# A two-layer MoE behind attention: the second layer's tokens in two blocks (1024, 512) in place of three of 512

## Chip, cores and metric

One core of a Trainium2 chip runs the whole kernel in one launch. The metric is the device time of one execution in microseconds (us). TensorE (PE) multiplies, VectorE (DVE), ScalarE (ACT) and GpSimd (POOL) work element by element, SyncE (SP) issues the DMAs.

## The reference, cut to what matters

```python
def reference(...):
    x = _attn_ref(q, k, v, centroids)      # 2 x 8 heads, 768 tokens, 64 wide, masked by cluster
    x = x.transpose(0, 2, 1, 3).reshape(1536, 512)
    x = _moe_ref(x, w_in, w_out)           # layer one: elu(x @ w_in) @ w_out, 512 -> 2048 -> 512
    return _moe2_ref(x, domain_probs, w1, w2)

def _moe2_ref(x, domain_probs, w1, w2):    # layer two: 4 experts, each 512 -> 1024 -> 512
    p = domain_probs / (domain_probs.sum(-1, keepdims=True) + 1e-09)
    for e in range(4):
        h = np.maximum(x @ w1[e], 0.0)
        out += p[:, e:e + 1] * (h @ w2[e])
```

## The kernel before

All matrix products take fp32 operands split in a high part and a rest (both fp32r); a product is three matmuls: high by high, high by rest, rest by high. The kernel has three stages: attention (to about 390 us), layer one (`moe`, to about 540) and layer two (to the end). The order of instructions on each engine is the order in which the code emits them.

Both layers are a list `steps`. Layer one has 48 steps, numbered 0 to 47: 16 chunks of 128 features, in groups of 2, 4, 5 and 5 chunks, each group for the three token blocks of 512 in turn; the last five steps of block 0, 1 and 2 end at step 37, 42 and 47. A step is a first product (`emit_G1`, two steps ahead) and a second one (`emit_G2`). When a block has its last step, `acc[tb]` (512 tokens, channels in four tiles of 128) is layer two's input.

Layer two has 16 chunks of 256 features (four per expert), and in the version before 3 steps to a chunk, one for each block of 512 tokens. Its first product is a Strassen form (Winograd's): features, channels and tokens are halved, and seven products take the place of eight. `x2_make` makes a block's seven inputs A11, A12, A22, S1 to S4 (high part on ACT, rest on POOL or DVE, called low here), `w2_split` a chunk's weights. I call one of the seven products a pass: two halves of 128 channels by three matmuls, six matmuls into a PSUM bank. `quad_early` does passes one to five (into the banks px, pz, px, py, px), `quad_late` the sixth (px) and seventh (pz). ACT copies px out between passes (m1, u2, u3), DVE adds up the quarters (c11, c2, c1). A quarter's relu goes to ACT (h), the rest of it to DVE (l). So h0 is the first 128 features, h1 the second; a stands for the first half of the tokens, b for the second. The two products of neighbouring steps are laced: passes one to five of the next step, tile 0 of this step's second product, passes six and seven, tiles 1 to 3. A tile is 128 tokens: six matmuls of 512 columns, and then an eviction on DVE, which adds the PSUM bank, times `prob`, to `acc`. Five PSUM banks (`ps_a`) rotate over the tiles.

While layer one ends, `tick` walks through generators (`going`) piece by piece: a block's inputs, and the next chunk's weights. Before, blocks 0 and 1 have theirs made while layer one still runs, and block 2 during layer two's first steps.

Of the kernel before, what the change touches and what calls it, by code (L numbers as in the profile page):

```python
# [46 lines left out]
def kernel(  # L47
# [30 lines left out]
    ident = const.tile([128, 128], F32, name="ident")  # L78
    identb = const.tile([128, 128], BF16, name="identb")
    ramp = const.tile([128, 1, 2 * C], F32, name="ramp")  # L80
    cc = const.tile([128, HP, 4 * C], F32R, name="cc")
# [22 lines left out]
    def attention():  # L104
# [27 lines left out]

        kscale = fix.tile([4 * C, 1], F32, name="kscale")
# [485 lines left out]
    W2_TAGS = (early[:6], last[1:7])  # L619
    X2_TAGS = (  # L620
        ["qh", "ql", "kl"] + [f"x0{kk}" for kk in range(KD)],
        [f"x1{kk}" for kk in range(KD)] + early[6:] + last[:1],
        [f"x2{kk}" for kk in range(KD)] + last[7:],
    )
    A11, A12, A22, S1, S2, S3, S4 = range(7)
# [48 lines left out]
    def w2_split(n):  # L674
# [14 lines left out]
        for x, names in (  # L689
            (a[:, :, 0], ("B11", "B21")), (t[:, 0:2].rearrange("p a k f -> p (a k) f"), ("T1", "T2")),  # L690
            (t[:, 2:4].rearrange("p a k f -> p (a k) f"), ("T3", "T4")), (b22, ("B22",)),
        ):
            m = 2 * len(names)
            o = home(tags[len(ops) // 2], [128, 2, m, 128], "w1op")
# [4 lines left out]
        h, l = (home(tag, [128, 2, 512], "w2op") for tag in tags[4:])  # L699
# [46 lines left out]
    def moe():  # L746
# [8 lines left out]
        g_t, x2, x2_gen, w_gen2 = {}, {}, {}, {}  # L755

        def emit_G1(s):
# [12 lines left out]
            gh = gp.tile([128, 512], F32R, tag="gh", name="gh")  # L770
            gl = gp.tile([128, 512], F32R, tag="gl", name="gl")
            r = tp.tile([128, 512], F32, tag="r", name="r")
            gg = tp.tile([128, 512], F32, tag="gg", name="gg")
# [8 lines left out]
        def product(ps, a, b, s, start, stop):  # L782
            tb, n = steps[s][1:3]
            x, w = x2[tb][a], w_t[n][0][b]
# [7 lines left out]
        def quad_early(s):  # L792
            px, py, pz = (ps_h.tile([128, 256], F32, tag=f"h{i}", name="h") for i in range(3))
            u = [tp.tile([128, 2, 256], F32, tag=t, name=t) for t in ("r", "gg")]
            c = tp.tile([128, 512], F32, tag="r", name="c")
            m1, u2, u3, c11 = u[0][:, 0], u[0][:, 1], u[1][:, 0], u[1][:, 1]
# [9 lines left out]
            dve.tensor_tensor(out=c[:, 256:512], in0=pz, in1=u3, op=ALU.add)  # L806
            more(s, 2)
            return px, pz, u2, c11, c

        def more(s, n):  # L810

            if s == NS1 + 1:
                for _ in range(n):
                    next(x2_gen[NB - 1], None)

        def quad_late(s, px, pz, u2, c11, c):
            a, b = slice(0, 256), slice(256, 512)
            (h0, l0), (h1, l1) = g_t[s] = [
                (gp.tile([128, 512], F32R, tag="gh", name="gh"), gp.tile([128, 512], F32R, tag="gl", name="gl"))
                for _ in range(2)  # L820
            ]
            act.activation(out=h0[:, a], in_=c11, func=AF.Relu)
            product(px, A22, "T4", s, False, True)
            product(pz, S4, "B22", s, False, True)
            act.activation(out=h0[:, b], in_=px, func=AF.Relu)
# [6 lines left out]
            low(l0[:, a], h0[:, a], c11)  # L832
            low(l0[:, b], h0[:, b], px)
            more(s, 2)
            dve.tensor_tensor(out=c[:, a], in0=pz, in1=u2, op=ALU.add)
            act.activation(out=h1, in_=c, func=AF.Relu)
            low(l1, h1, c)
            more(s, 2)

        def x2_make(tb, t):  # L840
# [3 lines left out]
            x2[tb] = {}  # L844
            ends = tb == NB - 1
            if ends:

                o = moe_p["st"].tile([128, 2, 512, 2], I32, tag="st", name="st").bitcast(F32)
                o = o.rearrange("p i f t -> p (i f t)").rearrange("p (n k f) -> p n k f", n=4, k=2)
                sums = [o[:, n] for n in range(4)]  # L850

            def high(i, x):
                o = home(X2_TAGS[tb][i], [128, 2, 2, 256], "x2")
                x2[tb][i] = o[:, 0], o[:, 1]
                act.activation(out=o[:, 0], in_=x, func=AF.Copy)

            def low(i, x):
                h, l = x2[tb][i]
                if ends or i not in (S1, S2, S4):
                    pool.tensor_tensor(l, x, h.bitcast(F32), ALU.subtract)  # L860
                else:
                    dve.tensor_tensor(out=l, in0=x, in1=h.bitcast(F32), op=ALU.subtract)

            def both(i, x):
                high(i, x)
                low(i, x)

            def sum_of(x, y, op):
                o = sums.pop() if ends else tp.tile([128, 2, 256], F32, tag="xs", name="xs")
                dve.tensor_tensor(out=o, in0=x, in1=y, op=op)  # L870
                return o

            s1 = sum_of(a21, a22, ALU.add)
            if ends:

                s2 = sum_of(a11, s1, ALU.subtract)
                yield
                high(A11, a11)
                high(S1, s1)
                yield  # L880
                low(A11, a11)
                low(S1, s1)
                s4 = sum_of(a12, s2, ALU.add)
                yield
                high(S2, s2)
                high(A12, a12)
                yield
                low(S2, s2)
                s3 = sum_of(a11, a21, ALU.subtract)
                low(A12, a12)  # L890
                yield
                high(S3, s3)
                high(A22, a22)
                high(S4, s4)
                yield
                low(S3, s3)
                low(A22, a22)
                low(S4, s4)
                return
            both(A11, a11)  # L900
            yield
            s2 = sum_of(a11, s1, ALU.subtract)
            both(S1, s1)
            yield
            both(S2, s2)
            yield
            s4 = sum_of(a12, s2, ALU.add)
            both(A12, a12)
            yield
            s3 = sum_of(a11, a21, ALU.subtract)  # L910
            both(S4, s4)
            yield
            both(A22, a22)
            yield
            both(S3, s3)
# [3 lines left out]
        def emit_G2(s, ms=range(4)):  # L919
            ly, tb, n, opens, closes, first, final = steps[s]  # L920
            if opens and 0 in ms:
# [88 lines left out]
        for t in sorted(load_at):  # L1010
            if t < -2 * LAG:
                for n in load_at[t]:
                    w_load(n)
# [63 lines left out]
```

## Time and profile before

| | |
|---|---|
| median of 3 runs | 1048.33 us (1048.17 to 1050.28) |
| profiled execution, span from first to last instruction | 1049.3 us; its own time is not listed apart from the three runs |
| TensorE busy | 1030.4 us of it |
| VectorE, ScalarE, GpSimd busy | 737.4, 525.2, 397.5 us |
| matmuls | 6265 |

The span leaves out what lies ahead of the first and behind the last instruction on the chip; here it is 1.0 us above the median of the runs, and within their spread. A busy TensorE is not a TensorE at its peak: a matmul of 256 columns that waits for its weights counts as busy.

### The profile page before, as it was taken

Reading aid. Unit: us, or ns where it says so; the run is one execution under the profiler, and the core shown is the slowest. Engines: PE = TensorE matmul, PEld = TensorE weight load, DVE = VectorE, ACT = ScalarE, POOL = GpSimd, SP = SyncE. Lnnn points to the kernel's source line nnn. Section 1 sums busy time; section 2 is a strip of 40 time slices with the busy share of each in tenths; the row PEclk is TensorE's granted clock in tenths of the full one; section 3 lists DMA queues with packets and bytes.
Section 4 is the critical chain, followed back from the end, with each engine's and each line's share of the span. In section 5 each row is a group of like instructions: output and inputs, shape, how many; then the busy total and the mean of one; then the engine's idle time right before and its main releaser. Section 6 shows DMA issues by size and latency. Waiting matters only on the chain.

```text
span 1049.3 us, 16463 instructions
## 1 busy us (share of the span) xinstructions
PE 1030.4 (98%) x6265; PEld 919.9 (88%) x6265; DVE 737.4 (70%) x1243; ACT 525.2 (50%) x1081; POOL 397.5 (38%) x398
## 2 busy tenths in 40 slices
PE   8999999999999999999999999999999999999998
PEld 7989999989877888888888899999989898989897
DVE  6999999898679674325576765666666767666665
ACT  3989999988777554224443332333332333332331
POOL 4878888979688766344641000000000000000000
PEclk8999999999999999999999999999999999999999
DMA  5846554430333222010002101111101111001003
GB/s 138 195 108 161 139 128 113 122 90 5 128 112 122 81 85 77 1 41 0 1 1 81 41 1 41 41 41 41 40 3 41 41 41 41 13 29 41 1 1 121
DMA packets 61469, 66.74 MB, mean 64 GB/s; under 512 B 28944, under 2 KB 47376, under 8 KB 61392
## 3 DMA queue, kind: packets, MB, share of 16 engines
q1 hardware_dynamic: 61392, 65.71, 22.1%
q8 instruction: 49, 0.80, 0.3%
q14 instruction: 28, 0.23, 0.1%
HBM read 43.08 MB, written 3.15 MB: 44 GB/s over the span
## 4 chain that ended last, share of the span: by engine, by line
PE 81%; DVE 7%; POOL 5%; ACT 4%; issue 2%; DMA 1%; POOLq 0%; DVEq 0%; ACTq 0%; SPq 0%
PE a L937 35%; PE h L787 23%; PE h L767 10%; PE x L456 3%; PE tps L423 3%; POOL p L411 2%; PE s L375 2%; PE s L378 2%; DVE pl L444 1%; DVE nm L384 1%; POOL xT L488 1%; PE warm L524 1%; DVE wa L732 1%; PE qkps L199 1%; ACT e L393 1%
## 5 line engine op out<-in xcount | busy, mean ns | idle before, releaser
L787 PEld LDWEIGHTS h<-x,w1op 128*128 128x128 f32 x2016 | 257.5, 190 | 10.2 <-ACT r L798 1.2
L787 PE MATMUL h<-x,w1op 128*128 128x256 f32 x2016 | 261.2, 285 | 1.0 <-ACT r L798 1.0
L937 PE MATMUL a<-w2op,gh 128*128 128x512 f32 x768 | 238.6, 392 | 0.0
L937 PEld LDWEIGHTS a<-w2op,gh 128*128 128x128 f32 x768 | 138.0, 188 | 23.8
L946 DVE SCALAR_TENSOR_TENSOR acc<-a,prob,acc 128x512 f32<-128x512 f32 x180 | 129.7, 747 | 40.1 <-PE a L937 40.1
L937 PE MATMUL a<-w2op,gl 128*128 128x512 f32 x384 | 149.5, 389 | 0.0
L767 PE MATMUL h<-xT,wh 128*128 128x512 f32 x384 | 118.5, 390 | 0.6 <-DVE gg L776 0.5
L411 POOL TENSOR_SCALAR p<-e,sm 128x768 f32<-128x768 f32 x96 | 89.2, 936 | 36.7 <-DVE sm L405 26.7
L776 DVE SCALAR_TENSOR_TENSOR gg<-r,h 128x512 f32<-128x512 f32 x48 | 32.9, 685 | 96.4 <-ACT r L775 74.9
L384 DVE TENSOR_REDUCE nm<-s 128x1 f32<-128x768 f32 x96 | 90.9, 947 | 2.8 <-PE s L378 2.6
L393 ACT ACTIVATE e<-s,nm 128x768 f32<-128x768 f32 x96 | 86.6, 902 | 4.5 <-POOL p L411 3.3
L423 PE MATMUL tps<-ident,p 128*128 128x128 f32 x576 | 83.8, 277 | 3.3 <-DVE pl L444 3.1
L767 PEld LDWEIGHTS h<-xT,wh 128*128 128x128 f32 x384 | 71.8, 188 | 16.2 <-DVE gg L776 1.5
L798 ACT ACTIVATE r<-h 128x256 f32<-128x256 f32 x48 | 18.5, 385 | 134.7 <-PE h L787 134.7
L937 PEld LDWEIGHTS a<-w2op,gl 128*128 128x128 f32 x384 | 72.1, 188 | 15.7
L444 DVE TENSOR_TENSOR pl<-tps,ph 128x512 fp32r<-128x512 f32 x112 | 76.3, 684 | 6.5 <-ACT ph L436 5.0
L774 ACT ACTIVATE r<-h 128x512 f32<-128x512 f32 x48 | 28.6, 596 | 97.5 <-PE h L767 96.8
L456 PE MATMUL x<-ph,v 128*128 128x256 f32 x288 | 76.5, 298 | 0.1
L777 POOL TENSOR_SCALAR gh<-gg 128x512 fp32r<-128x512 f32 x48 | 41.2, 858 | 91.8 <-DVE gg L776 90.9
L937 PE MATMUL a<-gh,wh 128*128 128x512 f32 x192 | 74.9, 390 | 1.0 <-ACT acc L953 0.9
L937 PE MATMUL a<-gl,wh 128*128 128x512 f32 x192 | 74.8, 390 | 0.0
L937 PE MATMUL a<-gh,wl 128*128 128x512 f32 x192 | 74.7, 389 | 0.0
(155 smaller groups left out, 1952.0 us busy)
## 6 DMA issues: line engine op xcount, KB each, us to landing
st<-in_moe_w_dram SPq DMA_DIRECT2D x32, 512.0 KB, 4.3
st<-in_moe_w_in_dram SPq DMA_DIRECT2D x14, 512.0 KB, 3.8
st<-in_moe_w_out_dram SPq DMA_DIRECT2D x14, 512.0 KB, 4.6
QA<-qh SPq DMA_DIRECT2D x30, 192.0 KB, 3.8
nq<-in_q_dram SPq DMA_DIRECT2D x16, 192.0 KB, 3.6
nk<-in_k_dram SPq DMA_DIRECT2D x16, 192.0 KB, 3.4
nv<-in_v_dram SPq DMA_DIRECT2D x8, 384.0 KB, 3.9
QB<-ql SPq DMA_DIRECT2D x16, 192.0 KB, 3.8
```

Source lines behind the costliest of these rows:

```text
L384: dve.tensor_reduce(out=m_t[w][:, i:i + 1], in_=s_t[HALF * w + i][:, :, 0:384], axis=AX.XY, op=ALU.max, negate=True)
L393: act.activation(out=e, in_=s_t.pop(u)[:, :, 0:384], func=AF.Exp, bias=m_t[w][:, i:i + 1], accum_out=e_t[w][0][:, i:i + 1])
L411: pool.tensor_scalar(p, e_t[w][1 + i].rearrange("p a b -> p (a b)"), e_t[w][0][:, i:i + 1], 1.0, ALU.mult, ALU.mult)
L423: pe.transpose(ps[:, x, :], p_t[w][i][:, c * 128:(c + 1) * 128], ident)
L444: dve.tensor_tensor(out=l, in0=ps, in1=h.bitcast(F32), op=ALU.subtract)
L456: pe.matmul(x_t[w], lhsT=v2[j][:, r, c, :], rhs=t[:, :, c, :], start=(c == 0 and t is ph[w]), stop=(c == T - 1 and t is pl[w]),)
L767: pe.matmul(ps, lhsT=w[:, 0, f], rhs=x, start=(kk == 0 and i == 0), stop=(kk == KD - 1 and i == 2))
L776: dve.scalar_tensor_tensor(out=gg, in0=r, scalar=-1.0, in1=ps, op0=ALU.add, op1=ALU.max)
L777: pool.tensor_scalar(gh, gg, 1.0, 0.0, ALU.mult, ALU.add)
L787: pe.matmul(ps, lhsT=w[wz][kk], rhs=x[xz][:, kk], start=(start and kk + i == 0), stop=(stop and kk == 1 and i == 2), skip_group_check=True,)
L937: pe.matmul(ps, lhsT=x, rhs=y, start=(opens and i == 0), stop=(closes and i == len(ops) - 1))
L946: dve.scalar_tensor_tensor(out=t, in0=ps, scalar=pr, in1=t, op0=ALU.mult, op1=ALU.add)
```

## The change

Layer two's blocks are now 1024 tokens (tiles 0 to 7, called wide here) and 512 (tiles 8 to 11, narrow). The wide block's two Strassen token halves are layer one's blocks 0 and 1, so its passes have 512 columns; the narrow block's have 256, as all had. A chunk has two steps in place of three. `x2_first` makes what needs block 0 alone (A11, A12), `x2_second` the other five once block 1 is there, `x2_last` the narrow block's. A wide step writes four pairs of h and l, 128 x 512 each, and `g_pair` gives them out of five buffers in turn (four in layer one). All scratch tiles come from one pool of six. `quad_late` stops for a wide block before h1a and l1a, which are made later. The loop over layer two is written out anew. Four constants of attention move into a pool that ends with it, to make room.

The diff, cut to its core:

```diff
-    for i in range(NP):
-        for tb in range(NB):
-            steps.append((2, tb, NC1 + i, True, True, i == 0, i == NP - 1))
+    BLOCKS = ((0, 8), (8, 4))
+    for i in range(NP):
+        for blk in range(len(BLOCKS)):
+            steps.append((2, blk, NC1 + i, True, True, i == 0, i == NP - 1))
...
-        gp = P("gp", 4)
-        tp = P("tp", 2)
+        gp = P("gp", 1)
+        tp = P("tp", 6)
...
+        def g_pair(ly):
+            out = []
+            for z, (nm, n) in enumerate((("gh", 5), ("gl", 5))):
+                k = turn[z] = (turn[z] + 1) % (n if ly == 2 else 4)
+                if (z, k) == (1, 4):
+                    out.append(home(G_TAG, [128, 512], nm))
+                else:
+                    out.append(gp.tile([128, 512], F32R, tag=f"{nm}{k}", name=nm))
+            return out
...
         def quad_early(s):
-            px, py, pz = (ps_h.tile([128, 256], F32, tag=f"h{i}", name="h") for i in range(3))
+            big = steps[s][1] == 0
+            n = 512 if big else 256
+            px, py, pz = (ps_h.tile([128, n], F32, tag=f"h{i}", name="h") for i in range(3))
...
+        def quad_late(s, px, pz, u2, c11, c1, c2):
+            big = steps[s][1] == 0
+            if big:
+                (h0a, l0a), (h1b, l1b), (h0b, l0b), (h1a, l1a) = (g_pair(2) for _ in range(4))
...
+            dve.tensor_tensor(out=c1, in0=pz, in1=u2, op=ALU.add)
+            if big:
+                yield
+                act.activation(out=h1a, in_=c1, func=AF.Relu)
+                low(l1a, h1a, c1)
...
+        def x2_second(t0, t1):
+            a11, a12, a21, a22 = t0[:, 0:2], t0[:, 2:4], t1[:, 0:2], t1[:, 2:4]
+            p0, p1 = sums_of(512)
+            dve.tensor_tensor(out=p0, in0=a21, in1=a22, op=ALU.add)
+            dve.tensor_tensor(out=p1, in0=a11, in1=p0, op=ALU.subtract)
+            yield
+            high(0, S1, p0, 512)
+            low(0, S1, p0, dve)
+            yield
+            high(0, S2, p1, 512)
+            low(0, S2, p1, pool)
+            yield
+            dve.tensor_tensor(out=p0, in0=a11, in1=a21, op=ALU.subtract)
+            high(0, S3, p0, 512)
+            yield
+            low(0, S3, p0, dve)
+            high(0, A22, a22, 512)
+            yield
+            low(0, A22, a22, pool)
+            dve.tensor_tensor(out=p1, in0=a12, in1=p1, op=ALU.add)
+            yield
+            high(0, S4, p1, 512)
+            low(0, S4, p1, dve)
+            yield
...
+        for s in range(NS1, NS, 2):
+            n = steps[s][2]
+            if n + 2 < NC1 + NP:
+                w_load(n + 2)
+            if s == NS1:
+                for m in range(8):
+                    emit_G2(s, (m,))
+                    next(x2_gen[1][0], None)
+                    advance()
+                ready(s + 1)
+                run_all(quad_late(s + 1, *quad_early(s + 1)))
+            else:
+                ready(s + 1)
+                q = quad_early(s + 1)
+                for m in range(4):
+                    emit_G2(s, (m,))
+                    advance()
+                run_all(quad_late(s + 1, *q))
+                for m in range(4, 8):
+                    emit_G2(s, (m,))
+                    advance()
+            g_t.pop(s)
+            if s + 2 < NS:
+                ready(s + 2)
+                q = quad_early(s + 2)
+                emit_G2(s + 1, (0,))
+                late = quad_late(s + 2, *q)
+                next(late)
+            if n + 2 < NC1 + NP:
+                w_gen2[n + 2] = w_split(n + 2)
+                going.append(w_gen2[n + 2])
+            for m in range(1 if s + 2 < NS else 0, 4):
+                advance(2)
+                emit_G2(s + 1, (m,))
+            if s + 2 < NS:
+                run_all(late)
+            g_t.pop(s + 1)
```

How that moves instructions is seen in two places. The first is TensorE in the middle of layer two, before: one pass a row (h is the product's bank, x an input, w1op the split weights), behind it a tile of the second product (a its bank, gh and gl the relu's high part and rest, w2op the weights), and passes six and seven.

```order
L787 MATMUL h<-x_6611,w1op 128x256 x6
L787 MATMUL h<-x_6613,w1op 128x256 x6
L787 MATMUL h<-x_6650,w1op 128x256 x6
L787 MATMUL h<-x_6652,w1op 128x256 x6
L787 MATMUL h<-x_6660,w1op 128x256 x6
L937 MATMUL a<-w2op,gh 128x512 x2
L937 MATMUL a<-w2op,gl 128x512
L937 MATMUL a<-w2op,gh 128x512 x2
L937 MATMUL a<-w2op,gl 128x512
L787 MATMUL h<-x_6662,w1op 128x256 x6
L787 MATMUL h<-x_6664,w1op 128x256 x6
```

The same engine now, at the end of a wide block's seventh pass; a pass has two input tiles here (x_6438 high, x_6439 rest), so its six matmuls are several rows.

```order
L811 MATMUL h<-x_6438,w1op 128x512
L811 MATMUL h<-x_6439,w1op 128x512
L811 MATMUL h<-x_6438,w1op 128x512 x2
L811 MATMUL h<-x_6439,w1op 128x512
L811 MATMUL h<-x_6438,w1op 128x512
L990 MATMUL a<-w2op,gh 128x512 x2
L990 MATMUL a<-w2op,gl 128x512
```

Two thirds of the passes before are now half as many, with twice the columns; the second product's matmuls have the form that they had. The narrow block's passes look as all did.

The second place is VectorE where layer two begins, before: it makes the weights of chunk 17 (w1op, w2op) and the third block's inputs between the first evictions (L944), with a step's quarters (L803, L806, L828, L835) among them.

```order
L670 TENSOR_TENSOR w1op<-T,w1op 128x512
L670 TENSOR_TENSOR w1op<-st,w1op 128x256
L944 TENSOR_SCALAR acc<-a,prob 128x512 x3
L803 TENSOR_TENSOR gg<-h,r 128x256
L806 TENSOR_TENSOR c<-h,gg 128x256
L944 TENSOR_SCALAR acc<-a,prob 128x512
```

Now, from l1a of the first wide block (the first row) over layer one's last additions (L1009) and the narrow block's sums (L940) to its first quarters (L832, L835):

```order
L850 SCALAR_TENSOR_TENSOR gl<-c,gh 128x512
L1009 TENSOR_TENSOR acc<-a,acc 128x512 x4
L940 TENSOR_TENSOR st<-acc 128x512
L940 TENSOR_TENSOR st<-acc,st 128x512
L676 TENSOR_TENSOR w1op<-T,w1op 128x512
L998 TENSOR_SCALAR acc<-a,prob 128x512 x2
L940 TENSOR_TENSOR st<-acc,st 128x512
L676 TENSOR_TENSOR w1op<-T,w1op 128x512
L998 TENSOR_SCALAR acc<-a,prob 128x512 x2
L940 TENSOR_TENSOR st<-acc 128x512
L676 TENSOR_TENSOR w1op<-st,w1op 128x256
L998 TENSOR_SCALAR acc<-a,prob 128x512 x2
```

Behind these stand the weight low of `w2op` (128x1024), the last two evictions, and then the narrow block's c11 and c2 (L832, L835). All eight evictions of the first wide step lie ahead of the narrow block's quarters, where before four evictions lay between one step's quarters and the next's.

## Rows read from the trace of the kernel before

**Rows 1.** The page: busy time, and two lines of the 40 slices.

```profile
PE 1030.4 (98%) x6265; PEld 919.9 (88%) x6265; DVE 737.4 (70%) x1243; ACT 525.2 (50%) x1081; POOL 397.5 (38%) x398
...
POOL 4878888979688766344641000000000000000000
PEclk8999999999999999999999999999999999999999
```

**Rows 2.** Windows: two runs of passes, second product, layer one (busy us, instructions).

```profile
core 0: us, PE busy (x) PEld busy (x) DVE busy (x) ACT busy (x) POOL busy (x), PEclk, DMA share, GB/s
753.43:757.11 3.68, 3.68 (x32) 3.65 (x30) 3.61 (x6) 0.81 (x3) 0.00 (x0) 1.00 0.00 0
758.50:759.93 1.43, 1.43 (x14) 1.43 (x12) 1.19 (x3) 0.39 (x1) 0.00 (x0) 1.00 1.05 371
759.93:764.03 4.10, 4.10 (x20) 3.38 (x19) 2.75 (x5) 0.64 (x1) 0.00 (x0) 1.00 0.22 84
409.81:412.53 2.72, 2.72 (x14) 2.25 (x12) 0.00 (x0) 0.00 (x0) 2.64 (x3) 1.00 0.02 6
```

**Rows 3.** Timeline of TensorE over one block: start, us, operation.

```profile
764.03 3.84 PE L787 MATMUL h<-x,w1op 128*128 128x256 f32 x30
...
769.10 1.59 PE L787 MATMUL h<-x,w1op 128*128 128x256 f32 x12
...
774.64 3.84 PE L787 MATMUL h<-x,w1op 128*128 128x256 f32 x30
```

**Rows 4.** Groups by line and form, 380 to 1049 us: busy us, mean ns, idle.

```profile
L946 DVE SCALAR_TENSOR_TENSOR acc<-a,prob,acc 128x512 f32<-128x512 f32 x180 | 129.7, 747 | 40.1 <-PE a L937 40.1
...
L828 DVE SCALAR_TENSOR_TENSOR gl<-c,gh 128x512 fp32r<-128x512 f32 x48 | 33.2, 693 | 33.6 <-ACT gh L836 33.6
L836 ACT ACTIVATE gh<-c 128x512 fp32r<-128x512 f32 x48 | 30.4, 634 | 40.1 <-DVE c L835 40.1
L670 DVE TENSOR_TENSOR w1op<-T,w1op 128x512 fp32r<-128x512 f32 x32 | 23.3, 727 | 1.4 <-ACT w1op L667 1.4
```

**Rows 5.** Timeline, the same block: ACT's first copy, DVE's first difference, the evictions behind.

```profile
765.01 0.39 ACT L798 ACTIVATE r<-h 128x256 f32<-128x256 f32 x1 [3.76 <-PE h L787]
...
772.50 0.42 DVE L682 TENSOR_TENSOR T<-st 128x256 f32<-128x256 f32 x1
...
773.96 2.06 DVE L946 SCALAR_TENSOR_TENSOR acc<-a,prob,acc 128x512 f32<-128x512 f32 x3
```

**Rows 6.** Timeline of TensorE where layer two begins; in brackets the wait ahead.

```profile
529.49 3.78 PE L787 MATMUL h<-x,w1op 128*128 128x256 f32 x30
...
533.80 1.70 PE L787 MATMUL h<-x,w1op 128*128 128x256 f32 x12
...
553.32 2.44 PE L787 MATMUL h<-x,w1op 128*128 128x256 f32 x18 [0.99 <-ACT r L798]
```

**Rows 7.** Timeline of DVE and POOL there: first and last POOL low, DVE beside them.

```profile
545.05 1.62 POOL L860 TENSOR_TENSOR x<-acc,x 128x512 fp32r<-128x512 f32 x1 [12.07 <-ACT x L855]
...
547.20 1.45 DVE L870 TENSOR_TENSOR st<-acc 128x512 f32<-128x512 f32 x1
...
551.78 1.56 DVE L670 TENSOR_TENSOR w1op<-T,w1op 128x512 fp32r<-128x512 f32 x1 [1.39 <-ACT w1op L667]
...
554.45 1.48 POOL L860 TENSOR_TENSOR x<-st,x 128x512 fp32r<-128x512 f32 x1
...
554.69 2.06 DVE L944 TENSOR_SCALAR acc<-a,prob 128x512 f32<-128x512 f32 x3
```

**Rows 8.** Timeline of DVE as block 1 ends; two groups of 1024 elements.

```profile
512.61 2.48 DVE L955 TENSOR_TENSOR acc<-a,acc 128x512 f32<-128x512 f32 x4
...
515.00 2.20 DVE L670 TENSOR_TENSOR w2op<-st,w2op 128x1024 fp32r<-128x1024 f32 x1
...
L670 DVE TENSOR_TENSOR w2op<-st,w2op 128x1024 fp32r<-128x1024 f32 x16 | 20.5, 1282 | 0.0
...
L743 POOL TENSOR_TENSOR wl<-wa,wh 128x1024 fp32r<-128x1024 f32 x5 | 14.0, 2800 | 0.0
```

More of the change, by code (lines that the diff above doesn't have):

```diff
@@ L698, in w2_split @@
             yield
-        h, l = (home(tag, [128, 2, 512], "w2op") for tag in tags[4:])
+        h, l = (home(tag, [128, 2, 512], "w2op") for tag in tags[3:])
         b = b.rearrange("p (c d) -> p c d", c=2)
@@ L769, in emit_G1 @@
                     )
[L770 to L773, printed above, removed]
+            gh, gl = g_pair(1)
+            r, gg = (scratch([128, 512], nm) for nm in ("r", "gg"))
             act.activation(out=r, in_=ps, func=AF.Relu, scale=-1.0)
@@ L805, in quad_early @@
             act.activation(out=u3, in_=px, func=AF.Copy)
[L806 to L825, printed above, removed]
+            dve.tensor_tensor(out=c2, in0=pz, in1=u3, op=ALU.add)
+            return px, pz, u2, c11, c1, c2 if big else c
+        def quad_late(s, px, pz, u2, c11, c1, c2):
+            big = steps[s][1] == 0
+            if big:
+                (h0a, l0a), (h1b, l1b), (h0b, l0b), (h1a, l1a) = (g_pair(2) for _ in range(4))
+                g_t[s] = [((h0a, h0b), (l0a, l0b)), ((h1a, h1b), (l1a, l1b))]
+            else:
+                (h0, l0), (h1, l1) = (g_pair(2) for _ in range(2))
+                a, b = slice(0, 256), slice(256, 512)
+                h0a, l0a, h0b, l0b = h0[:, a], l0[:, a], h0[:, b], l0[:, b]
+                g_t[s] = [((h0,), (l0,)), ((h1,), (l1,))]
             def low(l, h, x):
@@ L830, in low @@
                 )
[L832 to L840, printed above, removed]
+            act.activation(out=h0a, in_=c11, func=AF.Relu)
+            if big:
+                act.activation(out=h1b, in_=c2, func=AF.Relu)
+            product(px, A22, "T4", s, False, True)
@@ new lines, in quad_late @@
+            product(pz, S4, "B22", s, False, True)
+            act.activation(out=h0b, in_=px, func=AF.Relu)
+            low(l0a, h0a, c11)
+            if big:
+                low(l1b, h1b, c2)
+            low(l0b, h0b, px)
+            dve.tensor_tensor(out=c1, in0=pz, in1=u2, op=ALU.add)
+            if big:
+                yield
+                act.activation(out=h1a, in_=c1, func=AF.Relu)
+                low(l1a, h1a, c1)
+            else:
+                c = c2.rearrange("p a n -> p (a n)")
+                act.activation(out=h1, in_=c, func=AF.Relu)
+                low(l1, h1, c)
@@ new lines, in high, with low @@
+        def high(blk, i, x, n):
+            tags = X2_TAGS[blk][i]
+            if blk == 0:
+                x2[0][i] = [home(tag, [128, 2, n], "x2") for tag in tags]
+            else:
+                o = home(tags, [128, 2, 2, n], "x2")
+                x2[1][i] = o[:, 0], o[:, 1]
+            act.activation(out=x2[blk][i][0], in_=x, func=AF.Copy)
+        def low(blk, i, x, eng):
+            h, l = x2[blk][i]
+            if eng is pool:
+                pool.tensor_tensor(l, x, h.bitcast(F32), ALU.subtract)
+            else:
+                dve.tensor_tensor(out=l, in0=x, in1=h.bitcast(F32), op=ALU.subtract)
@@ new lines, in sums_of, with x2_first @@
+        def sums_of(n):
+            o = moe_p["st"].tile([128, 2, 512, 2], I32, tag="st", name="st").bitcast(F32)
+            o = o.rearrange("p i f t -> p (i f t)").rearrange("p (n k f) -> p n k f", k=2, f=n)
+            return [o[:, i] for i in range(2048 // (2 * n))]
+        def x2_first(t0):
+            a11, a12 = t0[:, 0:2], t0[:, 2:4]
+            high(0, A11, a11, 512)
+            yield
+            low(0, A11, a11, pool)
+            yield
+            yield
+            high(0, A12, a12, 512)
+            yield
+            low(0, A12, a12, pool)
+            yield
@@ L842, in x2_make, with x2_last @@
+        def x2_last(t):
             a, b = slice(0, 256), slice(256, 512)
             a11, a12, a21, a22 = t[:, 0:2, a], t[:, 2:4, a], t[:, 0:2, b], t[:, 2:4, b]
[L844 to L869, printed above, removed]
-                dve.tensor_tensor(out=o, in0=x, in1=y, op=op)
-                return o
@@ L873, in x2_make @@
[L873 to L899, printed above, removed]
@@ L914, in x2_make @@
+            high(1, S4, s4, 256)
             yield
-            both(S3, s3)
+            low(1, S3, s3, pool)
+            low(1, A22, a22, pool)
+            low(1, S4, s4, pool)
         a_ps, acc = {}, {}
```

137 lines of the change are left out of this document (82 added, 55 removed).

## The prediction

> **What bounds the kernel now.** Start with the page: TensorE is busy in 98% of the span, at the full granted clock from the second slice on [rows 1]. So a change pays only where it shortens TensorE's own instructions or takes away one of its few waits; VectorE (DVE), ScalarE (ACT) and GpSimd (POOL) matter where they make TensorE wait. Next I cut one block of layer two into windows. Its 42 product matmuls of 256 columns stand in two runs, 30 in 3.68 us and 12 in 1.43 us: 5.11 us, 121.7 ns each. In both runs the weight loads are busy as long as the matmuls are (3.65 of 3.68, 1.43 of 1.43): with 256 columns the next weights come no faster than the matmul ends. The 512-column matmuls of the second product take 4.10 us for 18 (227.8 ns), and those of layer one 2.72 us for 12 (226.7 ns), with weight loads busy in 2.25 of 2.72 [rows 2]. Two 256-column matmuls cost 243.3 ns, one of 512 columns 226.8 ns. The timeline says that this repeats without a wait: a block starts at 764.03, the next at 774.64, 10.61 us later [rows 3].
>
> **Term 1, the products.** Per chunk there were three blocks of 42 matmuls with 256 columns; now there are 42 with 512 columns and 42 with 256. Columns and arithmetic stay. 42 x 16 chunks = 672 pairs of matmuls become one matmul each, worth 243.3 - 226.8 = 16.5 ns: 672 x 16.5 = 11.1 us. The 512-column price is taken from layer one, which is the same form (128x128 weights, 512 columns, fp32r, nothing late). Between 226.7 and 227.8 ns it moves the term by 0.7 us.
>
> **A rule against it.** The window rows say that a 256-column matmul pays for its weight load. The Trainium skill ("TensorE: Matmul & The Clock Gate", section "Back-to-back issue gap") gives a spacing of N/2.4 + 2.5 ns at full clock: by estimate 109.2 ns for 256 columns and 215.8 ns for 512. That is a saving of 2.6 ns a pair, 1.7 us in all, where the rows give 11.1. The trace disagrees with it: 121.7 and 226.8 ns.
>
> **Term 2, fewer changes of kind.** 24 second-product matmuls at 226.8 ns would be 5.44 us; a block shows 10.61 - 5.11 = 5.50. I put the 0.06 to its two changes from 256 columns to 512, 0.03 each. 96 such changes become 64: 0.7 us is what I take, after rounding down from 1.0; bounds 0 and 1.0.
>
> **What the other engines do per chunk, and why I cost it at nothing.** The work on DVE and ACT covers the same elements in fewer instructions. But a wide block's last half (h1a, l1a: second features, first tokens) is now made behind the narrow block's second product. Count from T0, the start of the wide block's sixth pass. TensorE: passes six and seven to 2.7, tiles 1 to 3 of the narrow block to 6.8, the next narrow block's five passes to 10.5, and the sixth matmul of the wide block's first tile, which reads l1a, at 11.6. DVE in its order, with 0.25 us from a matmul's end to a reader's start (the first ACT copy begins at 765.01, 0.98 after a pass of 0.73 began): c2 and an eviction to 1.05, three lows of 0.69, the third after h0b (2.2), to 3.1; c1 to 3.8; the four T differences take 1.46 (772.50 to 773.96) to 5.2; then three evictions of 0.75 with two weight lows of 0.73 between, the last not before tile 3 ends (6.8), to 8.9; l1a to 9.6 [rows 4, 5]. That is 2.0 us early. The other waits inside a chunk have more: a pass may start again on a PSUM bank once ACT has copied it (0.25 + 0.6 us), and between lies a pass of 1.36. Weights are loaded a chunk (31 us) ahead, and their splits end before the chunk starts.
>
> **Term 3, the change of layers.** Before, TensorE stalls here once for 0.99 us (a copy on ACT is late), and a run of 12 takes 0.1 longer [rows 6]; both go: 1.1 us. After, the first wide block's seven passes start at the same 529.49, and need both of layer one's first blocks.
> Its inputs: block 1 is summed by 515.1 (512.61 + 2.48). From there DVE has seven 1024-element operations and one weight low at 1.28 us, or up to 2.2 beside GpSimd, and some 3.8 us of others: 14 to 21 us, so S4 is done between 529 and 536. The seventh pass, which reads it, starts at 538.3. The two GpSimd lows of 2.8 us fit between. Hidden, if not by much [rows 8].
> Then h0b goes into the buffer of layer one's step 46 (47 mod 4 = 3), so it waits for that step's last matmul: 529.5 + 5 x 1.36 + 0.7 + 2.7 + 2.0 = 541.7. From there h0b, l0b, c1, h1a, l1a in a row end at 545.4; the wide block's first tile starts at 544.5 and wants l1a at 545.6. No stall, with 0.2 to spare.
> Then DVE is the one to watch. Before the bank of tile 2 is free for tile 7 it does four additions (2.5), two sums, a weight low, another sum, another weight low and three evictions. Alone these operations take about 0.7 us each; while GpSimd makes the last block's lows (545.05 to 555.9 in the trace, later by some 4 us now), a DVE operation with both operands in SBUF took 1.45 and 1.56 us instead; evictions from PSUM did not get longer, three in 2.06 [rows 7]. So tile 2 is evicted at 553.5 (all alone) or 556.1 (three of them slowed); tile 7 wants to start at 554.0: 0 or 2.1 us of stall. The narrow block behind it has its sixth pass right after its fifth, so it waits 0.25 + 0.4 us for ACT's copy (0.7); its seventh waits for c2, which stands on DVE behind five more evictions, a sum and two weight lows: 0, or 3.0 us slowed. The wide block behind needs this block's low: 0.7 or 0.8. In all 1.4 to 6.6 us. GpSimd is at work through nearly all of it, so I take 4.5, nearer the slowed end. Net of the 1.1: +3.4 (from +0.3 to +5.5).
>
> **Sum.** -11.1 - 0.7 + 3.4 = -8.4 us. The profiled span is 1049.3; its own time is not listed beside it, and the span lies 1.0 above the median of the three runs (1048.33), inside their spread. 1049.3 - 8.4 = 1040.9 as a span, 1039.9 against the median. I forecast 1039.9.
>
> **Rivals.**
> *Cheap change of layers (0.2).* DVE keeps pace, stalls 1.4 us: -11.1 - 1.0 + 0.3 = -11.8, 1036.5. For it: evictions keep their pace beside GpSimd. Against: the two slowed rows [rows 7].
> *Dear change of layers (0.12).* DVE is so late that the first wide block's passes wait too, or the stalls pass 6.6 us; each microsecond is one. With 8 to 9 us of stalls: 1043 to 1045. For it: the 2 us left before the seventh pass.
> *Slower, because l1a comes late in every chunk (0.06).* TensorE then waits at the sixth matmul of each wide block's first tile, fifteen times. It eats the gain from 0.6 us of waiting a chunk (8.4 / 15), so with l1a 2.6 us later than worked out; from 2.7 us on it is slower by over 0.2% ((8.4 + 2.1) / 15 = 0.7). At 3.5 us it would be 1.5 x 15 = 22 us, 1062. Against: GpSimd does nothing in the later slices [rows 1], so DVE's rows of the steady stretch should hold.
> *The columns alone set a matmul's time (0.04).* Then a 512-column product costs two of 256 (243.3 ns), term 1 is nothing, and -0.7 + 3.4 gives 1051.0. By the spacing that the Trainium skill states ("TensorE: Matmul & The Clock Gate", the same section) it would be 1.7 us less, 1049.3. Against: layer one's 226.7 and the saturated weight loads.
>
> **How the numbers follow.** The forecast's own case has 0.58, with 1038 to 1042. A measurement here can tell from no change what is over about 0.2%, 2.1 us. The first three cases (0.90) are faster by more, but for some 0.02 of the dear one; the late l1a and the columns rival go 0.03 to the same and 0.07 to slower: faster 0.88, same 0.05, slower 0.07. The range 1036.4 to 1044.2 leaves out the two dear tails and the end of the dear change of layers, and reaches to the cheap end of every term.
>
> **What the profile after would show.** Right: the 42 wide passes at 227 ns a matmul with weight loads no longer saturated; a chunk of about 31.1 us (9.53 + 5.11 + 16.4) against 3 x 10.61 = 31.8; no wait before the second product in the steady chunks; TensorE's waits together near 545 to 566, put down to VectorE. Wrong: a wait on the low of line 850 in every chunk; wide passes above 235 ns; or stalls at the change of layers well past 7 us.

## The result, and the profile after

The changed kernel takes 1039.27 us (median of 5 runs, 1038.34 to 1039.35), the kernel before 1048.33 (5 runs by now, 1047.21 to 1051.70). The ratio is 0.990, 95% interval 0.9886 to 0.9915: faster by 9.1 us. The forecast was 1039.9.

The profiled execution has a span of 1037.4 us. Its page begins:

```profile
PE 1016.8 (98%) x5593; PEld 881.9 (85%) x5593; DVE 724.1 (70%) x1156; ACT 513.2 (49%) x994; POOL 396.1 (38%) x394
```

Against [rows 1], TensorE has 672 matmuls fewer and 13.6 us less of work; its share stays at 98%. The spans differ by 11.9 us, more than the medians do, and part of that is not the change: layer two's first pass starts at 526.98, not at 529.49 [rows 6], though the code ahead of it does the same work. In all twelve profiles of this study that start lies between 526.1 and 529.8, whatever the kernel; what moves it isn't shown. So I compare kernels by **layer two's time**, from its first pass to the end of the span: 1049.3 - 529.5 = 519.8 us before, 1037.4 - 527.0 = 510.4 after, **9.4 us less**. A second profile of the changed kernel gives 510.4 again.

The windows of the changed kernel: passes one to five and six and seven of a wide block, passes one and two and then three and four of a narrow one, and a whole chunk.

```profile
core 0: us, PE busy (x) PEld busy (x) DVE busy (x) ACT busy (x) POOL busy (x), PEclk, DMA share, GB/s
779.93:786.73 6.80, 6.80 (x31) 5.63 (x30) 1.47 (x3) 1.20 (x2) 0.00 (x0) 1.00 0.46 155
788.10:790.81 2.71, 2.71 (x13) 2.25 (x12) 2.67 (x5) 1.76 (x4) 0.00 (x0) 1.00 0.03 6
...
763.89:765.32 1.43, 1.43 (x14) 1.41 (x12) 1.43 (x4) 0.39 (x1) 0.00 (x0) 1.00 0.00 0
765.32:766.84 1.52, 1.52 (x15) 1.52 (x13) 0.62 (x2) 0.38 (x1) 0.00 (x0) 1.00 0.00 0
...
763.89:794.89 31.00, 31.00 (x157) 26.49 (x156) 20.32 (x35) 9.58 (x18) 0.00 (x0) 1.00 0.10 35
```

A wide pass has 6.80 / 30 = 226.7 ns a matmul, and its weight loads are busy in 5.63 of 6.80 us, no longer all the time as in [rows 2]. A chunk takes 31.00 us, against 3 x 10.61 = 31.83 [rows 3]: 0.83 less, 13 us in 16 chunks. That is 4 us more than the whole gain, so the change of layers costs 4 us. All that TensorE waits for in layer two stands there:

```profile
engine line waited for: us in total, times, longest us
PE a L990 <- DVE acc L998: 1.4, 1, 1.4
PE h L811 <- ACT u L827: 1.1, 1, 1.1
PE h L811 <- ACT u L834: 0.5, 1, 0.5
PE h L811 <- DVE gl L850: 0.2, 1, 0.2
```

The timeline of TensorE shows where: tile 7 of the first wide block, then the narrow block's third and sixth pass, then the second chunk's wide block. The last row is that chunk's narrow block, from which on every chunk is like the next.

```profile
526.98 6.96 PE L811 MATMUL h<-x,w1op 128*128 128x512 f32 x30
...
551.88 0.39 PE L990 MATMUL a<-w2op,gl 128*128 128x512 f32 x1
553.64 0.73 PE L990 MATMUL a<-w2op,gh 128*128 128x512 f32 x2 [1.38 <-DVE acc L998]
...
557.88 2.43 PE L811 MATMUL h<-x,w1op 128*128 128x256 f32 x18 [1.15 <-ACT u L827]
560.85 1.69 PE L811 MATMUL h<-x,w1op 128*128 128x256 f32 x12 [0.53 <-ACT u L834]
562.76 7.09 PE L811 MATMUL h<-x,w1op 128*128 128x512 f32 x30 [0.22 <-DVE gl L850]
...
577.85 3.84 PE L811 MATMUL h<-x,w1op 128*128 128x256 f32 x30
```

From 526.98 to 577.85 are 50.9 us. The matmuls in between (24 of layer one, 84 wide products and 72 of the second product at 226.8 ns, 42 narrow ones in 5.11 us) take 45.9. So 4.9 us are lost here, 3.3 of them listed as waits; the rest is mostly what it takes to start again behind a wait (tile 7 starts 1.53 us after its turn, listed are 1.38), and two gaps of 0.2 that the list leaves out.

What VectorE (DVE), GpSimd (POOL) and ScalarE (ACT) did meanwhile, three timelines of the same stretch:

```profile
545.59 1.35 DVE L940 TENSOR_TENSOR st<-acc 128x512 f32<-128x512 f32 x1
...
548.19 1.40 DVE L998 TENSOR_SCALAR acc<-a,prob 128x512 f32<-128x512 f32 x2
549.51 1.72 DVE L940 TENSOR_TENSOR st<-acc,st 128x512 f32<-128x512 f32 x1
551.15 1.78 DVE L676 TENSOR_TENSOR w1op<-T,w1op 128x512 fp32r<-128x512 f32 x1
552.85 1.40 DVE L998 TENSOR_SCALAR acc<-a,prob 128x512 f32<-128x512 f32 x2
...
545.10 1.29 POOL L886 TENSOR_TENSOR x<-acc,x 128x512 fp32r<-128x512 f32 x1 [11.64 <-ACT x L881]
547.68 2.99 POOL L886 TENSOR_TENSOR x<-st,x 128x512 fp32r<-128x512 f32 x2 [1.30 <-ACT x L881]
550.62 1.76 POOL L886 TENSOR_TENSOR x<-acc,x 128x512 fp32r<-128x512 f32 x1
...
556.52 1.04 ACT L673 ACTIVATE w2op<-st 128x1024 fp32r<-128x1024 f32 x1
557.47 0.36 ACT L827 ACTIVATE u<-h 128x256 f32<-128x256 f32 x1
```

Ahead of the eviction of tile 2 (552.85) VectorE has a sum and a weight subtraction of 1.72 and 1.78 us, where 0.69 is usual. And ScalarE's copy of the first narrow pass (L827, at 557.47) stands behind a weight copy of 1.04 us.

### The profile page after: what moved, and what is told of

The parts are those of the page before. It is cut to its first block, busy times and chain, and to the rows that moved or that the text cites. A ratio compares the mean times of both kernels' runs of the same rounds, so it can differ in the third digit from the quotient of the medians.

```text
span 1037.4 us, 14919 instructions
## 1 busy us (share of the span) xinstructions
PE 1016.8 (98%) x5593; PEld 881.9 (85%) x5593; DVE 724.1 (70%) x1156; ACT 513.2 (49%) x994; POOL 396.1 (38%) x394
## 4 chain that ended last, share of the span: by engine, by line
PE 82%; DVE 8%; ACT 3%; POOL 2%; DMA 2%; issue 2%; SPq 0%; DVEq 0%; ACTq 0%; POOLq 0%
PE a L990 35%; PE h L811 22%; PE h L793 11%; PE x L456 4%; PE tps L423 4%; PE s L375 2%; PE s L378 2%; DVE pl L444 1%; POOL p L411 1%; DVE nm L384 1%; DMA KA<-kh 1%; PE qkps L199 1%; DVE wa L743 1%; PE warm L524 1%; DVE wa L737 1%
## 5 line engine op out<-in xcount | busy, mean ns | idle before, releaser
L811 PE MATMUL h<-x,w1op 128*128 128x512 f32 (+1 forms) x1344 | 245.0, 337 | 2.0 <-ACT u L827 1.1
L811 PEld LDWEIGHTS h<-x,w1op 128*128 128x128 f32 x1344 | 211.7, 189 | 31.8 <-ACT u L827 1.4
L990 PEld LDWEIGHTS a<-w2op,gh 128*128 128x128 f32 x768 | 142.1, 188 | 30.2 <-DVE acc L998 1.8
L1000 DVE SCALAR_TENSOR_TENSOR acc<-a,prob,acc 128x512 f32<-128x512 f32 x180 | 134.4, 748 | 34.3 <-PE a L990 34.1
L793 PE MATMUL h<-xT,wl 128*128 128x512 f32 x192 | 74.7, 389 | 0.0
```

Of the source, the lines that this page charges most:

```text
L793: pe.matmul(ps, lhsT=w[:, 0, f], rhs=x, start=(kk == 0 and i == 0), stop=(kk == KD - 1 and i == 2))
L811: pe.matmul(ps, lhsT=w[wz][kk], rhs=x[xz][:, kk], start=(start and kk + i == 0), stop=(stop and kk == 1 and i == 2), skip_group_check=True,)
L990: pe.matmul(ps, lhsT=x, rhs=y, start=(opens and i == 0), stop=(closes and i == len(ops) - 1))
L1000: dve.scalar_tensor_tensor(out=t, in0=ps, scalar=pr, in1=t, op0=ALU.mult, op1=ALU.add)
```

## The experiments

My theory: the gain is the price of 256-column matmuls and of the changes between 256 and 512; the loss is VectorE held up by GpSimd, and a queue on ScalarE. The rivals: the columns alone set a matmul's time, and the new order gains; or VectorE's order of work makes the waits, and GpSimd has no part in them. "Layer two" is the measure explained above; the ratio is to the kernel before, run beside.

| run | median us | ratio, 95% interval | first pass, span | layer two us |
|---|---|---|---|---|
| e0_after | 1040.01 | 0.991 (0.9893 to 0.9928) | 526.78, 1037.15 | 510.4 |
| e1_halves | 1049.20 | 1.000 (0.9994 to 1.0012) | 526.35, 1046.23 | 519.9 |
| e2_quiet_pool | 1036.83 | 0.989 (0.9872 to 0.9903) | 528.61, 1036.23 | 507.6 |
| e3_w2op_late | 1038.20 | 0.990 (0.9886 to 0.9913) | 527.53, 1036.96 | 509.4 |
| e4_w1op_late | 1036.48 | 0.989 (0.9873 to 0.9904) | 529.75, 1037.55 | 507.8 |
| e5_laced | 1038.43 | 0.990 (0.9880 to 0.9916) | 526.08, 1034.46 | 508.4 |
| e6_before_spread | 1044.81 | 0.996 (0.9941 to 0.9972) | 527.25, 1043.29 | 516.0 |
| e7_l1a_late | 1062.49 | 1.013 (1.0112 to 1.0153) | 527.61, 1060.68 | 533.1 |
| e8_s4_behind | 1035.44 | 0.987 (0.9847 to 0.9887) | 527.54, 1034.68 | 507.1 |
| e9_all | 1035.15 | 0.986 (0.9847 to 0.9882) | 527.68, 1033.81 | 506.1 |

**The changed kernel again (e0_after).** 

> The changed kernel again, unaltered, beside the other runs of this call. It should take 1039.3 us, with 510.4 us from layer two's first pass to the end of the span and a chunk of 31.0.

Layer two took 510.4 us, with the same four waits and a chunk of 31.0. The median is 1040.01, 0.7 more than expected and inside the spread of its six runs (1037.92 to 1041.52).

**Wide passes in halves (e1_halves).**

```diff
-            for kk in range(2):
-                for i, (wz, xz) in enumerate(((0, 0), (0, 1), (1, 0))):
-                    pe.matmul(ps, lhsT=w[wz][kk], rhs=x[xz][:, kk], ...
+            for c in (slice(0, 256), slice(256, 512))[:2 - blk]:
+                for kk in range(2):
+                    for i, (wz, xz) in enumerate(((0, 0), (0, 1), (1, 0))):
+                        pe.matmul(ps[:, c], lhsT=w[wz][kk], rhs=x[xz][:, kk, c], ...
```

> Every matmul of a wide pass becomes two of 256 columns (all six of a pass for the first half of the tokens, then all six for the second); blocks, buffers, the order of everything else and the change of layers stay as in the changed kernel. My theory: the gain is the price of 256-column matmuls, 672 x 16.5 ns = 11.1 us, and the changes from 256 to 512 columns, 64 of them at 0.03 us = 1.9 us (the wide passes have none, which I had miscounted in the forecast as 32 more). So a chunk goes from 31.0 back to 31.8 us and the time up by about 13.0 us, to 1052. With the forecast's count of changes (0.7 us) it would go up by 11.8, and a chunk to 31.74. Rival, the columns alone set a matmul's time and the gain is the new order: no change, a chunk stays at 31.0.

(The two halves share a PSUM bank, each with a start flag of its own, and the wide block's sums come out wrong; all matmuls are issued.) The time goes back to about that of before, so the new order by itself does not make the gain, and the rival falls. But it rises by 9.5 us in layer two, not by 13.0 or 11.8. The windows: a wide block's first five passes, and a chunk.

```profile
783.99:791.18 7.19, 7.19 (x61) 7.18 (x60) 1.47 (x3) 1.20 (x2) 0.00 (x0) 1.00 0.41 147
...
767.95:799.55 31.60, 31.60 (x199) 28.68 (x198) 20.34 (x35) 9.58 (x18) 0.00 (x0) 1.00 0.10 34
```

A matmul of 256 columns takes 7.19 / 60 = 119.8 ns here, not 121.7, and a chunk 31.60 us, 0.60 more than after and 0.23 less than before. So a part of what I took for a matmul's price is something else, which two short passes in a row have and two long ones don't. A small share of the gain, 0.23 of 0.83 us a chunk, does come without wider matmuls. The next run looks for it.

**The passes spread (e6_before_spread).**

```diff
+            if not spread:
+                p2()                       # the pass with T2 into px, and its copy u2
             product(py, A12, "B21", s, True, True)
             dve.tensor_tensor(out=c11, in0=py, in1=m1, op=ALU.add)
+            if spread:                     # tile 0 follows, then T3 into px,
+                p2()                       # tile 1, T4 and B22, tiles 2 and 3
```

> The kernel before, with the order of a block's passes altered from the third block on: the pass with B21 goes ahead of that with T2, the pass with T3 behind tile 0 and the pair T4, B22 behind tile 1; so no pass writes px directly after the copy of a pass one step before. Nothing is left out. My theory: of the 121.7 ns that I took as the price of a 256-column matmul a part is no price: the run of 30 takes 3.68 us where 30 matmuls at 119.7 would take 3.59, since the third and the fifth pass wait 0.08 and 0.02 us for ScalarE's copy of px, which is too short for the profile's list of waits. These waits go (0.1 a block) and one more change from 256 to 512 columns comes (0.03): -0.07 x 46 blocks = -3.4 us, 1045, and 3 blocks in 31.6 us in place of 31.8. Rival, the 0.1 us belongs to the run of 30 itself (five changes of bank or of inputs): no gain, and 0.03 x 46 = 1.4 us more.

Layer two takes 516.0 us, 3.7 less than before, and the median is 1044.81: the theory holds. Three blocks take 31.62 us in place of 31.83, 0.07 less each, so 3.2 of the 3.7 us stand in the 46 altered blocks. The rest stands at the change of layers, where the wait of 0.99 us for ScalarE's copy [rows 6] is 0.3 in this run. The windows show the effect, first two stretches of the kernel before (passes one and two, then three and four of a block), and then, in the altered order, passes one to four (24 matmuls) and three blocks.

```profile
764.03:765.46 1.43, 1.43 (x13) 1.40 (x12) 0.75 (x1) 0.39 (x1) 0.00 (x0) 1.00 0.00 0
765.46:766.98 1.52, 1.52 (x14) 1.52 (x13) 0.00 (x0) 0.39 (x1) 0.00 (x0) 1.00 0.00 0
```

```profile
770.35:773.22 2.87, 2.87 (x26) 2.87 (x24) 2.47 (x5) 0.39 (x1) 0.00 (x0) 1.00 0.03 6
...
753.53:785.15 31.62, 31.62 (x200) 28.60 (x198) 21.06 (x39) 10.13 (x23) 0.00 (x0) 1.00 0.10 34
```

24 matmuls in 2.87 us are 119.6 ns each, with three changes of bank among them, so the rival falls. In the order of before, passes three and four lose 0.09 us, since px is still being copied when pass three wants it. What waits is the weight load at the head of pass three: by the spacing of the loads ahead of it (0.12) its turn is at about 765.35, the copy ends at 765.40 (765.01 + 0.39, [rows 5]), and the load starts at 765.44:

```profile
765.44 0.19 PEld L787 LDWEIGHTS h<-x,w1op 128*128 128x128 f32 x1
```

TensorE counts as busy meanwhile, and no list of waits has it.

**GpSimd quiet (e2_quiet_pool).**

```diff
-                x2[1][i] = o[:, 0], o[:, 1]
+                x2[1][i] = o[:, 0], o[:, 0]
...
             h, l = x2[blk][i]
+            if blk == 1:
+                return
```

> Leaves out the rest (low part) of the narrow block's seven inputs: GpSimd's seven subtractions at the change of layers are gone, and the products read the high part a second time; TensorE does as many matmuls as before. My theory: VectorE's operations with both operands in SBUF are slowed by GpSimd beside them (1.35 to 1.78 us in place of 0.69), and that makes tile 7 wait for the eviction of tile 2 and ScalarE's copy stand behind a late weight copy. Without GpSimd they take 0.7 us, both waits (1.5 and 1.3 us) go, the narrow block's sixth pass still waits for a copy, and the time falls by about 3 us, to 1036.3. Rival, the order of VectorE's list alone makes the waits, GpSimd has no part: durations stay, and so do the waits of TensorE, within 0.5 us.

Layer two falls by 2.8 us. VectorE's timeline: the third sum, the weight subtraction behind it, the evictions of tiles 2 and 3.

```profile
550.49 0.68 DVE L942 TENSOR_TENSOR st<-acc,st 128x512 f32<-128x512 f32 x1
551.09 0.68 DVE L676 TENSOR_TENSOR w1op<-T,w1op 128x512 fp32r<-128x512 f32 x1
551.69 1.40 DVE L1000 TENSOR_SCALAR acc<-a,prob 128x512 f32<-128x512 f32 x2
```

The order is the same, the durations are 0.68 in place of 1.72 and 1.78, and TensorE's waits for tile 7 and for the copy L827 are gone from its list. The rival falls. In the changed kernel no wait of TensorE is put down to GpSimd's own results, so what this run takes away is VectorE's delay.

**The weights of the next chunk later (e3_w2op_late, e4_w1op_late).** Nothing is left out: the first keeps the last weight split (`w2op`) behind the narrow block's products, the second also those of T3, T4 and B22.

```diff
                 for m in range(8):
                     emit_G2(s, (m,))
                     next(x2_gen[1][0], None)
-                    advance()
+                    advance(1 if m < 4 else 0)     # e4: m < 1
```

> Only the split of chunk 17's second weights (ScalarE 1.04 us, VectorE 1.66 us) is moved behind the narrow block's first products at the change of layers; nothing is left out. My theory: the copy m1 of the narrow block stands behind this weight copy on ScalarE, 1.15 us on TensorE; it goes, the wait for tile 2's eviction stays, and the last of GpSimd's subtractions (to 560.4) gives back some 0.3: -0.8 us, 1038.4. Rival, the copy is late for the products' own latency or because inputs are late: no change.

> As the run with the second weights moved, and the splits of the weights T3, T4 and B22 of chunk 17 move behind the narrow block's products as well; nothing is left out. My theory: a weight subtraction of 1.78 us on VectorE no longer stands ahead of the evictions of tiles 2 and 3, so tile 7 starts without its wait of 1.5 us, the third input's sum comes 1.8 us earlier, and ScalarE's copy is not late: -2.4 us, 1036.8. Rival, GpSimd's subtractions (to 560.4) set when the narrow block can end: not over 0.8 us, as in the run before; and the weights moved could be late for the next wide block, a wait at its fifth pass.

Layer two falls by 1.0 and by 2.6 us (expected 0.8 and 2.4). In the first the wait for L827 shrinks from 1.1 to 0.2 and tile 7 still waits (1.3); in the second tile 7 doesn't wait either. TensorE's list in the second:

```profile
PE h L811 <- ACT u L834: 0.5, 1, 0.5
PE h L811 <- DVE gl L850: 0.2, 1, 0.2
PE h L811 <- ACT u L827: 0.2, 1, 0.2
```

So GpSimd holds VectorE up, but taking the next chunk's weights out of VectorE's and ScalarE's queues there does as much as silencing it.

**Tile 7 between the passes (e5_laced), and S4 behind the copies (e8_s4_behind).** Both begin from e4_w1op_late, and `x2_last` makes its sum S3 ahead of S4; the loop's other edits:

```diff
-                for m in range(8):
+                for m in range(7):
                     emit_G2(s, (m,))
-                    next(x2_gen[1][0], None)
+                    if m < 5:                      # e8 only: S4's copy is left for ready()
+                        next(x2_gen[1][0], None)
-                ready(s + 1)
-                run_all(quad_late(s + 1, *quad_early(s + 1)))
+                q = quad_early(s + 1)
+                ready(s + 1)                       # e5: ahead of quad_early
+                emit_G2(s, (7,))
+                run_all(quad_late(s + 1, *q))
```

> As the run with T3, T4 and B22 moved; besides, the narrow block's third sum S3 is made ahead of S4, so VectorE and ScalarE give it to GpSimd before two evictions and not behind them, and tile 7 stands between the narrow block's fifth and sixth pass at the change of layers. Nothing is left out. My theory: of the 4.9 us lost at the change of layers 2.3 are left after that run (copies between passes 0.2 and 0.5, the low of h0 0.2, the rest latencies); tile 7 covers the copy ahead of the sixth pass (0.7) and the wait for S4's rest: -1.2 us against that run's 507.8 us of layer two, 506.6, and 1035.3 in all. Rival, ScalarE's copies of the inputs stand ahead of m1 and the third pass waits for it as much as is won: 507.8.

The rival came true: 508.4, 0.6 more than without the lacing. ScalarE's and TensorE's timelines:

```profile
553.38 0.63 ACT L881 ACTIVATE x<-st 128x512 fp32r<-128x512 f32 x1 [1.80 <-DVE st L940]
553.92 0.36 ACT L827 ACTIVATE u<-h 128x256 f32<-128x256 f32 x1
...
554.34 2.43 PE L811 MATMUL h<-x,w1op 128*128 128x256 f32 x18 [1.54 <-ACT u L827]
```

ScalarE waits 1.80 us for VectorE's fourth sum, and the copy for which TensorE waits stands behind. So the next run moves it:

> As the run with tile 7 laced in, and ScalarE's copy of the fourth sum S4 (and GpSimd's rest of it) now stand behind the copies m1, u2 and u3 of the narrow block, not ahead of them; nothing is left out. My theory: in that run m1 stood behind S4's copy, which waited for VectorE's sum behind three evictions, and TensorE waited 1.5 us; this wait goes, and S4's rest is done before the seventh pass, since tile 7 and the sixth pass lie between: 506.9 us from layer two's first pass to the end, against 508.4 in that run and 510.4 in the changed kernel; 1036 in all. Rival, S4's rest comes late for the seventh pass and the wait moves there: 508.

507.1 us; the narrow block's wait for L827 is gone, and 0.2 us of the rival's wait is there (the second row). The first row is a wait of the wide block behind it, for its own copy m.

```profile
PE h L811 <- ACT m L827: 0.2, 1, 0.2
PE h L811 <- POOL x L886: 0.2, 1, 0.2
```

**Both (e9_all).** The same as e8_s4_behind, with the altered order of e6_before_spread in the narrow blocks.

> As the run with S4 behind, and in 15 of the 16 chunks the narrow block's passes in the altered order that was tried on the kernel before: B21 ahead of T2, tile 0 of the wide block between the passes with T2 and T3. Nothing is left out. My theory: the short waits for ScalarE's copies (0.1 us a narrow block) go and one more change from 256 to 512 columns comes (0.03): -0.07 x 15 = -1.1 us, 505.8 us of layer two, a chunk in 30.93 us, and 1035 in all. Rival, tile 0 now comes a pass earlier, and l1a or an eviction is late for it: a wait on the wide block's low in each chunk, no gain.

506.1 us, 1.0 less, a chunk in 30.94. This version takes 1035.15 us: ratio 0.986 where the changed kernel has 0.990 and 0.991, and no overlap of the intervals.

**l1a late (e7_l1a_late).**

```diff
                 act.activation(out=h1a, in_=c1, func=AF.Relu)
+                if s > NS1 + 2:
+                    for _ in range(6):
+                        low(l1b, h1b, c2)
                 low(l1a, h1a, c1)
```

> The changed kernel with VectorE making l1b six times more, directly ahead of l1a, in 14 of the 16 chunks (3.7 us of work more in each; nothing else altered). In the changed kernel's trace l1a ends at 796.95, and the sixth matmul of the wide block's first tile, which reads it, starts at about 799.7: my theory is that VectorE has 2.5 us to spare there, so TensorE waits 1.2 us in each of the 14 chunks, on the low of the wide block, and the time rises by 16 us, to 1055. Rival, the spare time lies elsewhere (the wait falls on another buffer earlier, for example on evictions that come late): over 25 us; or VectorE has more to spare than the order shows: no change.

Layer two rises by 22.7 us (16 expected), 1.6 in each of 14 chunks. The wait is where the rival "l1a late" put it: the fourteen first tiles, the list says, and the timelines of VectorE and TensorE show one of them.

```profile
PE a L993 <- DVE gl L850: 18.3, 14, 1.3
```

```profile
806.84 4.91 DVE L850 SCALAR_TENSOR_TENSOR gl<-c,gh 128x512 fp32r<-128x512 f32 x7
...
811.80 0.50 PE L993 MATMUL a<-w2op,gl 128*128 128x512 f32 x1 [1.34 <-DVE gl L850]
```

Seven lows take 4.91, so the six added cost 4.2 us and not the 3.7 that I had reckoned: 4.2 - 1.6 = 2.6 us is what VectorE had to spare, where the changed kernel's trace gave 2.5. Only the size of the load was off.

## Why the prediction was right, step by step

**Term 1, the products: right in its sum, half wrong in its reason.** I forecast 11.1 us as 672 pairs of matmuls at 16.5 ns. The price of a 256-column matmul is 119.7, not 121.7, so a pair gives 2 x 119.7 - 226.8 = 12.6 ns, 8.5 us in all. The 0.09 us by which 30 matmuls exceed that price is the wait for px, and the change takes it from 32 of 48 blocks: 2.9 us. Together 11.4. A wide pass takes 1.36 us, so the copy (0.25 us to its start and 0.6) is done in time; I had said so of the new passes, and not seen that the old ones, of 0.73 us, were too short for it. Why 256 columns take 119.7 ns, more than half of the 226.7 for 512, no run shows: weight loads that are busy all the time (7.18 of 7.19 us in e1_halves) fit, but none was changed.

By the spacing that the Trainium skill states ("TensorE: Matmul & The Clock Gate", section "Back-to-back issue gap"), e1_halves would, by estimate, be 1.7 us slower than the changed kernel. The section gives that spacing for a matmul by itself, and says that it counts too little at small N, for want of the weight load, and too much at large N. The runs disagree with the spacing at both: e1_halves was 9.5 us slower in layer two, 256 columns take 119.7 ns (109.2 by estimate), and 512 take 226.7 (215.8), more and not less.

**Term 2, the changes from 256 to 512 columns: mis-sized, by a wrong count.** I had 96 to 64 and took 0.7. Wide passes have 512 columns, so only the narrow block's two a chunk are left: 96 to 32. At 0.03 each that is 1.9 us. In e1_halves a chunk gains two such changes, and 0.60 - 42 x 0.0126 = 0.07 us is left for them, 0.035 each. With term 1 that makes 13.3 us, and the chunk's 0.83 us say 13.3 too.

**The steady chunk: right.** No listed wait in it, though the narrow block's passes still lose 0.09 us behind px, as the old ones did (1.52 us for passes three and four, 1.43 for one and two). A chunk takes 31.00 (forecast about 31.1; its own terms add up to 31.04). From T0 (788.10) l1a ends at 8.9 us (forecast 9.6) and its reader starts at 11.6 (11.6); by e7_l1a_late it is 2.6 us early (2.0).

**Term 3, the change of layers: right in size, half right in its places.** Taken 4.5, bounds 1.4 to 6.6; lost are 4.9. The kernel before loses 1.3 here by the same count (taken 1.1), net 3.6 against 3.4. That the size came out so near is in part luck: 4.5 was a choice inside wide bounds, and a wait that was forecast did not come while another, of 1.3 us, was not foreseen. All times here lie 2.5 us ahead of the forecast's, since the first pass starts that much earlier.
- S4's rest ends at 531.6 (forecast 529 to 536), in time; l1a ends at 543.2, its reader starts at 543.4 (forecast 545.4 and 545.6): both right.
- Tile 7 waits for the eviction of tile 2: 1.5 us (0 or 2.1). The reason, VectorE beside GpSimd, is shown by e2_quiet_pool.
- The sixth pass waits 0.8 for a copy (0.7), the next wide block 0.4 for the low (0.7 to 0.8).
- The seventh pass does not wait for c2 (0 or 3.0 forecast). In its place the third pass waits 1.3 us for ScalarE's copy, which stands behind a weight copy (e3_w2op_late). I had gone through VectorE's list there and not through ScalarE's. The sign named for the profile, waits put down to VectorE, holds for 1.6 of the 3.3 us listed; ScalarE has the other 1.7.

**The sum.** -13.3 + 3.6 = -9.7, measured in layer two -9.4, by the medians -9.1; forecast -8.4. The miss of term 2 (1.2 us) is most of the difference.

**The rivals.** Neither the cheap (stalls of 1.4 us) nor the dear change of layers (over 6.6) came: 4.9 are lost. The evictions kept their pace beside GpSimd, as the cheap one said, but the sums and weight subtractions ahead of them did not. The late l1a did not come either; e7_l1a_late shows that its place was right, and with 2.5 us to spare by the trace its slope fits (1.6 us for 1.7 of delay). "The columns alone" fell with e1_halves.

## What to carry to other kernels

A group of matmuls that counts as busy can hold waits of a tenth of a microsecond, listed nowhere: compare groups of different lengths (30 in 3.68 us, 12 in 1.43) before you divide. Where two stages meet, write out the queue of every engine that TensorE waits for, not of the busiest alone; what is not needed until later (the next chunk's weights) goes behind the copies that are. And count what a change leaves, kind by kind, as carefully as what it removes.

## What the runs showed of the hardware

VectorE's operations with both operands in SBUF don't run slower beside GpSimd, they wait for it. In the timelines above those of 512 elements end about 0.55 us after a GpSimd subtraction ends, whenever they began: the sum of 545.59 ends at 546.94, GpSimd at 546.39; that of 549.51 at 551.23, GpSimd at 550.67; the weight subtraction of 551.15 at 552.93, GpSimd at 552.38. Evictions, which read PSUM, take 0.7 us each beside the same subtractions (548.19).

What is left behind GpSimd's end goes with the elements. Two rows of the kernel before, and three of the changed kernel a little later than those above:

```profile
552.75 1.74 POOL L860 TENSOR_TENSOR x<-acc,x 128x512 fp32r<-128x512 f32 x1
553.26 1.51 DVE L670 TENSOR_TENSOR w1op<-st,w1op 128x256 fp32r<-128x256 f32 x1
...
556.90 1.26 POOL L886 TENSOR_TENSOR x<-acc,x 128x512 fp32r<-128x512 f32 x1
557.59 1.66 DVE L676 TENSOR_TENSOR w2op<-st,w2op 128x1024 fp32r<-128x1024 f32 x1 [1.09 <-ACT w2op L673]
558.13 2.26 POOL L886 TENSOR_TENSOR x<-st,x 128x512 fp32r<-128x512 f32 x1
```

With 256 elements VectorE ends 0.28 us after GpSimd (554.77 and 554.49), with 1024 it ends 1.09 after (559.25 and 558.16). GpSimd waits in the same way: the subtractions of 550.62 and 558.13, which begin beside such an operation, take 1.76 and 2.26 us in place of 1.26 to 1.29, and both end about 1.15 us after VectorE's.

The Trainium skill says this ("SBUF — State Buffer", section "SBUF: two separate sides"): the port pair that both engines use is an exclusive lock; of an operation of VectorE with two SBUF inputs and one of GpSimd that reads SBUF, the one that starts first has it to its end, and the other blocks. The trace agrees: such an operation costs what is left of GpSimd's, up to 1.1 us here (1.78 in place of 0.68). I had taken the two slowed rows [rows 7] for a pace.
